# Moving a left-query pass from one kind of segment to the next in a recurrent-memory attention kernel

## The chip, the cores and the metric

The kernel runs on one core of a Trainium2 chip. The metric is the device time of one execution in microseconds; of several runs the median is given. Five engines of the core work side by side and wait for each other by semaphores: PE multiplies matrices into PSUM, ACT and DVE do elementwise work and take results out of PSUM, POOL and SP here mostly start transfers (DMA), which 16 DMA engines carry out.

## The reference, cut to what matters

The input is layer-normalised. One branch is a dense layer with GELU (1024 to 3584 and back), computed first. The other branch is attention with a recurrent memory, and takes most of the time. The 2048 rows are cut into 64 segments of 32 rows. To each segment 8 memory rows are put in front; queries, keys and values of 32 heads of 128 are made of these 40 rows; after a masked softmax and the output product, the results of the 8 memory rows are the next segment's memory:

```python
for s in range(n_seg):
    h = concatenate([mem, x[s]])           # 8 + 32 rows of 1024
    q, k, v = h @ Wq, h @ Wk, h @ Wv       # 32 heads of 128
    p = softmax(where(mask, q @ k.T * scale, -1e9))
    o = (p @ v) @ Wo
    mem, out[s] = o[:8], o[8:]
```

So segments can't run side by side: the memory that comes out of one goes into the next. The four weight matrices, 8 MB each, pass through PE once for every segment.

## The kernel before, in words

*Rows.* A matmul of 32 rows on the left uses a quarter of PE's columns, and four such matmuls run side by side. The main tile of a segment therefore has 32 rows: 24 of its own rows (NX) and the 8 memory rows. The other 8 rows of each segment, the "left" rows (NL), need no memory for their queries, keys and values. Those of four segments (GRP) make a second tile of 32 rows, `hL`, and their products are made once for a group of four segments, ahead of the group that uses them. A segment's place in its group, `i4`, is its kind, 0 to 3.

*Weights.* The weights are cut into 64 units of 128x2048 (512 KB): 8 for each of the half passes K0, Q0, K1, Q1, V0, V1, and 16 for the output pass O. 46 units stay in SBUF. 18 are streamed in every segment (the S in `PLACED`): 16 come from HBM on SP's queue, one of them in part, and two are kept in four PSUM banks and copied out by DVE (`copy_bits`). Streamed units go through 6 buffers. `unit_done` starts the next transfer into a buffer as soon as PE has used what was in it, so SP's queue goes strictly in the order in which units are used, some six units ahead.

*A segment.* `half_pass` makes one half pass: for each of 8 units, `product` issues four matmuls side by side for the main tile and, where the pass also has left rows, four more with the same unit for `hL`, into a second PSUM bank. Only three PSUM banks, `acc`, go round for all these sums. Results are taken out by ACT or DVE and turned by DVE (`turn_k`, `turn_q`, `turn_qL`). Between the products, at places given in the dictionaries `at`, the attention of the two halves is woven in: `scores`, `exps`, `sums`, `values`. Then comes the output pass, which in kind 1 has 64 rows instead of 32 (`left_o`) and takes twice as long.

*Which left passes lie in which kind.* `left_k`, `left_q`, `left_v`: K0 and V1 in kind 3, K1 and V0 in the kind 0 that follows, Q0 in kind 1, Q1 in kind 2, all for the next group.

*The boundary.* At a segment's end the memory has to go from PSUM through DVE or ACT (L1134, L1130), through PE again (`put_mem`, L293), and through a DVE cast into the main tile (L297), before the next K0 pass can begin. In that time PE makes up to six left products ahead (`LEAD`, `lead_products`), of resident units alone, for the left pass of the next segment: three before `put_mem` and three after. They keep one of the three banks until that pass is done, and the pass then makes only the two products of streamed units. Before the change each of the four kinds has such products at its end: Q0, Q1, K0, K1.

*Left queries.* `turn_qL` puts the left queries of a half, for all four segments of the next group, into `qL[u]`. This tile still holds those of the current group, so `keep_q` first copies the slots still needed into a corner of the PSUM bank `mixed` (`qS`), and `q_left` fetches a segment's 8 rows from there or from `qL[u]`. Q0's queries are overwritten in kind 1, so slots 2 and 3 are kept; Q1's in kind 2, so slot 3.

*Order.* The engines run their instructions in the order of this program; nothing is rearranged by a scheduler.

Of the kernel before, what the change touches and what calls it, by code (L numbers as in the profile page):

```python
# [11 lines left out]
U32 = mybir.dt.uint32  # L12
# [26 lines left out]
NL = SEG - NX  # L39
GRP = 4  # L40
# [49 lines left out]
def kernel(  # L90
# [63 lines left out]
    def slab(place):  # L154
        if place in low:
            return low[place]
        return slabs.tile([P, 2048], BF16, name="u", tag=place)
# [3 lines left out]
    qL = [consts.tile([P, 16, SEG], BF16, name="qL"), qL_last]  # L161
# [6 lines left out]
    for j in range(4):  # L168
        q = slice(32 * j, 32 * j + 32)
# [73 lines left out]
    def copy_bits(out, in_):  # L243

        nc.vector.tensor_single_scalar(out=out, in_=in_, scalar=0, op=ALU.bitwise_or)  # L245
# [40 lines left out]
    def put_mem(o_sb, hT, ps, nb=4):  # L286

        nc_ = KT // nb
        rows = ident_mem[:, :, :] if nb == 4 else ident_mem[:, 1::2, :]
        psM = ps[:, 0:8 * KT].rearrange("p (c j t) -> p c j t", c=nc_, j=nb)  # L290
        for c in range(nc_):
            for q in range(4):
                nc.tensor.matmul(  # L293
                    psM[32 * q:32 * q + 32, c, :, :], lhsT=o_sb[:, 4 * c + q, :], rhs=rows,
                    start=(c == 0), stop=True, skip_group_check=True, tile_position=(0, 32 * q),
                )
        nc.vector.tensor_copy(  # L297
            out=hT[:, :, NX:SEG].rearrange("p (j c) t -> p j c t", c=nc_),
            in_=psM.rearrange("p c j t -> p j c t"),
        )  # L300
# [3 lines left out]
    with tc.tile_pool(name="ma", bufs=2) as ma, tc.tile_pool(name="mps", bufs=6, space=PSUM) as mps:  # L304
# [39 lines left out]
        for i in range(14):  # L344
            t = slab(f"w2_{i}")[:, :].rearrange("p (c d) -> p c d", d=DM)
# [174 lines left out]
        for tg in range(4):  # L520
            last = tg == 3
            if last:
# [3 lines left out]
                h = 4 * IN_BANKS[1] + 2 * IN_BANKS[2]  # L526
# [12 lines left out]
            for fb in range(FC):  # L539
# [10 lines left out]
                u = ma.tile([P, 512], BF16, name="g_u")  # L550
# [99 lines left out]
    with tc.tile_pool(name="late", bufs=1) as late, \  # L650
# [10 lines left out]
        def new_acc():  # L661
            bank = free_banks.popleft()
            ps = banks.tile([P, 512], F32, name="acc", tag=bank)
            bank_of[id(ps)] = bank, ps
            return ps
# [4 lines left out]
        mixed = banks.tile([P, 512], F32, name="mixed")  # L670
# [4 lines left out]
        qS = there[:, 0:32 * NL].rearrange("p (i h t) -> p i h t", i=2, h=16)  # L675
# [12 lines left out]
        def unit_tile(unit):  # L688
            nonlocal used
            if IS_STREAMED[unit]:  # L690
                place_in_stream[unit] = used
                used += 1
                return stream_tiles.pop(used - 1)[:, :]
            return res_tiles[unit]
# [25 lines left out]
        for s in range(NSEG):  # L720
            g, i4 = divmod(s, GRP)
            first, final = s == 0, s + 1 == NSEG
# [5 lines left out]

            more = g + 1 < NGRP
            left_k = [first or (i4 == 3 and more), i4 == 0]  # L730
            left_q = [first or (i4 == 1 and more), first or (i4 == 2 and more)]
            left_v = [i4 == 0, first or (i4 == 3 and more)]
            left_o = i4 == 1 or final
            og, slot = divmod(s + 2, GRP)
# [18 lines left out]
            def lead_products(n):  # L753

                w, u, psL, ahead, order = led["next"]
                for _ in range(n):
                    if led["made"] < len(ahead):
                        i = ahead[led["made"]]
                        product(w, i, res_tiles[w, i, u], hL, psL, order)
                        led["made"] += 1  # L760
# [63 lines left out]

            def q_left(u):

                if i4 >= 2 + u and more:
                    q = qS[:, i4 - 2 - u, :, :]
                else:
                    q = qL[u][:, :, NL * i4:NL * i4 + NL]  # L830
                nc.vector.tensor_copy(out=q_home[:, :, 0:NL], in_=q)
# [4 lines left out]

            def keep_q(u):

                n = 2 - u
                copy_bits(  # L840
                    mixed[:, 340:340 + 64 * n].bitcast(U32).rearrange("p (i h t) -> p h i t", i=n, h=16),
                    qL[u].bitcast(U32)[:, :, (GRP - n) * NL // 2:].rearrange("p h (i t) -> p h i t", i=n),
                )

            def scores(u):
# [170 lines left out]
            if first:  # L1016
                keep(IN_BANKS, 1024, d_oL, 2)
                keep(IN_BANKS, 0, half_home[:, 0:DM], 3)
                h = 4 * PART[1] + 2 * PART[2]
# [7 lines left out]
            if first:  # L1027
                turn_kL(psKL, 0)
            at = {} if first else {1: [lambda: q_left(0)]}
            if left_q[0] and not first:  # L1030
                at[2] = [lambda: keep_q(0)]
            psQ, psQL = half_pass("Q", 0, left_q[0], at)
            if first:
                turn_qL(psQL, 0)
                q_left(0)
            turn_q(psQ)
            if left_q[0] and not first:
                turn_qL(psQL, 0)
            psK1, psK1L = half_pass("K", 1, left_k[1], {7: [lambda: scores(0)]})
            exps(0, None if first else lambda: q_left(1))  # L1040
            st["kT", 1] = nat_home
            rows_out(psK1, nat_home, nc.scalar.copy)
# [5 lines left out]
            if left_q[1] and not first:  # L1048
                at[0].insert(0, lambda: keep_q(1))
# [60 lines left out]
            for n, unit in enumerate(O_UNITS):  # L1110
                t = unit_tile(unit)
# [13 lines left out]
            if not final:  # L1125
                o_sb = outM
                no = 16 if left_o else 8
                o = psX[:, 0:32 * no].rearrange("p (h e) -> p h e", e=32)
                if left_o:
                    nc.scalar.copy(out=o_sb[:, 0:no, :], in_=o)  # L1130
                else:
                    o = psX[:, 0:256].rearrange("p (h e) -> p h e", e=16)
                    flat = o_sb.rearrange("p h e -> p (h e)")[:, 0:256].rearrange("p (h e) -> p h e", e=16)
                    nc.vector.tensor_tensor(out=flat, in0=o, in1=st["folded"], op=ALU.add)  # L1134
                ahead = []
                if (i4 == 3 or more) and not final:
                    hL = nxt["hL"]
                    w, u = (("Q", 0), ("Q", 1), ("K", 0), ("K", 1))[i4]
                    ahead = [i for i in range(KT) if not IS_STREAMED[w, i, u]][:LEAD]
                    order = ahead + [i for i in range(KT) if i not in ahead]  # L1140
                    led.update(next=(w, u, new_acc(), ahead, order), made=0)
                    lead_products(LEAD // 2)
                put_mem(o_sb, nxt["hT"], mixed[:, 224:288], 4 // nw)
                if led:
                    lead_products(LEAD)
# [20 lines left out]
            if final:  # L1166
                engines = [nc.sync, nc.scalar]
                n = 0
# [57 lines left out]
```

## Time and profile before

| what | value |
|---|---|
| median of 3 runs | 1837.84 us (1831.92 to 1839.93) |
| profiled execution, its own time | 1834.89 us |
| its span, first to last instruction | 1833.2 us |
| PE busy | 1720.8 us, 94% |
| PE weight loads busy | 872.6 us, 48% |
| DVE busy | 962.2 us, 52% |
| ACT busy | 665.4 us, 36% |
| DMA queue of SP (weights) | 579.67 MB, 83.6% of 16 engines' span |
| granted PE clock | 0.998 |
| recurrent part | from about 417 us to the end |

A page of the profile covers one execution. Busy time is the union of an engine's instructions; matmuls overlap, and their ends are modelled. A row of a group of instructions names the line, the engine, the operation, and the tiles as out<-in. "Idle before" is how long the engine had stood still, and the arrow names what released it. The chain of work is followed back from the last instruction, at each step to what released it; a DMA's piece in it runs from its issue to its landing. In a stretch of time, the DMA share is the time that packets took, over 16 engines' time; it can come out a little over 1.

### The profile page before, as it was taken

What the parts mean: (1) busy time and instruction counts of PE and PEld (TensorE: products, weight loads), DVE (VectorE), ACT (ScalarE), POOL (GpSimd) and SP (SyncE); (2) the same over time, 40 slices, a digit from 0 to 9 for tenths busy, and PEclk for the clock granted to TensorE, in tenths of its full rate; (3) what the DMA queues carried; (4) which work ended last, traced back from release to release, by engine and by line L of the source; (5) the groups of instructions that cost most, each with busy time, mean ns of one, the idle gap of its engine ahead of it and who ended that gap; (6) DMA issues with size and microseconds to landing.
All of it is one profiled execution on the core that took longest, in us unless ns stands there. A gap on an engine that the chain in (4) does not pass through costs nothing.

```text
span 1833.2 us, 71272 instructions
## 1 busy us (share of the span) xinstructions
PE 1720.8 (94%) x31117; PEld 872.6 (48%) x31137; DVE 962.2 (52%) x2444; ACT 665.4 (36%) x1509; POOL 276.4 (15%) x542
## 2 busy tenths in 40 slices
PE   8999999998998999999999999999999999999997
PEld 4444444444444444554445545444445444444444
DVE  7657483805554545545455555555555454545543
ACT  6334251602333333333333334333333333333333
POOL 0000001500342111112111111111111111111111
PEclk9999999999999999999999999999999999999999
DMA  9921212769999999999999999999999999999997
GB/s 291 319 85 46 55 44 57 261 209 367 400 398 365 383 389 390 380 385 380 376 382 389 393 385 386 389 387 391 374 389 383 373 393 383 381 380 390 378 386 301
DMA packets 230821, 604.65 MB, mean 330 GB/s; under 512 B 46795, under 2 KB 86267, under 8 KB 230508
## 3 DMA queue, kind: packets, MB, share of 16 engines
q1 hardware_dynamic: 207252, 579.67, 83.6%
q0 software_dynamic: 16384, 16.64, 2.9%
q8 instruction: 244, 4.00, 0.9%
q10 hardware_dynamic: 6872, 3.78, 0.7%
q14 instruction: 69, 0.57, 0.1%
HBM read 586.02 MB, written 29.10 MB: 336 GB/s over the span
## 4 chain that ended last, share of the span: by engine, by line
PE 42%; DMA 22%; issue 3%; DVE 2%; ACT 1%; DVEq 0%; ACTq 0%; SPq 0%; POOLq 0%
PE acc L744 29%; DMA u<-Wc_V 10%; PE acc L991 9%; DMA u<-Wc_O 7%; DMA u<-Wc_Q 2%; DMA u<-Wc_K 2%; PE acc L934 1%; DVE d_oL L1012 1%; DVE u L245 1%; DMA hr_home<-hr_d 1%; PE mixed L853 1%; ACT mixed L897 1%; PE mixed L293 1%; PE mixed L859 0%; ACT q_all L1130 0%
## 5 line engine op out<-in xcount | busy, mean ns | idle before, releaser
L744 PE MATMUL acc<-u,hr_home 128*32 128x512 bf16 x11520 | 790.3, 380 | 43.7 <-DMA u<-Wc_V 17.5
L744 PEld LDWEIGHTS <-hr_home 128*32 128x32 bf16 x12288 | 334.1, 96 | 352.0 <-issue 60.2
L744 PE MATMUL acc<-u,hrL 128*32 128x512 bf16 x2880 | 247.2, 379 | 2.1 <-issue 1.0
L473 PE MATMUL ps<-u 128*128 128x512 bf16 (+1 forms) x920 | 194.4, 373 | 2.0 <-ACT u L390 2.0
L245 DVE TENSOR_SCALAR u<-kept 128x512 uint32<-128x512 uint32 x254 | 163.6, 686 | 62.0 <-PE acc L991 41.6
L795 ACT CAST d_oL<-acc 128x512 bf16<-128x512 f32 x128 | 74.6, 583 | 275.0 <-PE acc L744 275.0
L991 PE MATMUL acc<-u,q_all 128*32 128x256 bf16 (+1 forms) x2207 | 133.8, 300 | 20.0 <-DMA u<-Wc_O 15.0
L594 PE MATMUL ps<-u 128*128 128x512 bf16 x657 | 146.2, 379 | 0.8
L473 PEld LDWEIGHTS <-u 128*128 128x128 bf16 x920 | 89.8, 98 | 104.9 <-issue 2.4
L1188 POOL DMA_DIRECT2D out_dram<-hr_home x188 | 96.3, 513 | 260.8 <-DVE hr_home L1154 247.0
L991 PE MATMUL acc<-u,d_oL 128*32 128x512 bf16 (+1 forms) x1536 | 131.6, 382 | 1.2 <-DMA u<-Wc_O 0.7
L907 DVE TENSOR_TENSOR pd_main<-half_home,mixed 128x320 bf16<-128x320 bf16 x128 | 62.4, 488 | 132.2 <-ACT mixed L897 132.2
L809 DVE STREAM_TRANSPOSE q_all<-q_all 128x512 bf16<-128x512 bf16 x128 | 90.6, 708 | 71.1 <-ACT q_all L795 71.0
L991 PEld LDWEIGHTS <-q_all 128*32 128x32 bf16 x3381 | 99.8, 96 | 58.9 <-issue 27.9
L799 ACT CAST q_all<-acc 128x512 bf16<-128x512 f32 x128 | 75.2, 587 | 139.1 <-PE mixed L859 138.7
L267 POOL DMA_DIRECT2D hr_home<-hr_d x58 | 32.8, 565 | 591.0 <-PE acc L744 572.6
L744 PEld LDWEIGHTS <-hrL 128*32 128x32 bf16 x3072 | 84.9, 96 | 51.3 <-issue 7.6
L795 ACT CAST q_all<-acc 128x512 bf16<-128x512 f32 x128 | 75.2, 587 | 93.5 <-PE acc L744 93.5
L594 PEld LDWEIGHTS <-u 128*128 128x128 bf16 x672 | 65.3, 98 | 77.3 <-DVE g_u L555 0.4
L897 ACT ACTIVATE mixed<-mixed,small_consts 128x160 f32<-128x160 f32 x256 | 94.3, 368 | 8.4
L547 ACT ACTIVATE g_xb<-ps,b1col 128x512 bf16<-128x512 f32 x112 | 76.8, 686 | 55.5 <-PE ps L473 54.7
L991 PEld LDWEIGHTS <-d_oL 128*32 128x32 bf16 (+1 forms) x2048 | 65.5, 99 | 59.1 <-issue 12.2
(137 smaller groups left out, 2104.6 us busy)
## 6 DMA issues: line engine op xcount, KB each, us to landing
u<-Wc_K SPq DMA_DIRECT2D x256, 512.0 KB
u<-Wc_V SPq DMA_DIRECT2D x256, 512.0 KB
u<-Wc_O SPq DMA_DIRECT2D x256, 512.0 KB
u<-Wc_Q SPq DMA_DIRECT2D x192, 512.0 KB
u<-in_B_w_dram SPq DMA_DIRECT2D x28, 512.0 KB
u<-Wc_O SPq DMA_DIRECT2D x64, 192.0 KB
hr_home<-hr_d POOLq DMA_DIRECT2D x58, 128.0 KB, 5.3
u<-in_A_Wq_dram SPq DMA_DIRECT2D x13, 512.0 KB
```

The costliest lines, as they stand in the source:

```text
L245: nc.vector.tensor_single_scalar(out=out, in_=in_, scalar=0, op=ALU.bitwise_or)
L473: nc.tensor.matmul(ps[:, SEG * s0:SEG * s1].rearrange("p (s t) -> p s t", t=SEG), lhsT=w1_sb[fb // 2][:, kt, (fb % 2) * P:(fb % 2 + 1) * P ...
L547: nc.scalar.activation(out=xb[:, :], in_=ps[:, :], func=ACT.Identity, bias=b1col[:, fb:fb + 1], scale=1.0)
L594: nc.tensor.matmul(ps[:, :], lhsT=gts[fc // 4][:, fc % 4, t * P:(t + 1) * P], rhs=w2_sb[fc // 2][:, fc % 2, cs], start=(fc == 0), stop=(fc ...
L744: nc.tensor.matmul(o, lhsT=lhs[:, i, :], rhs=m, start=(i == seq[0]), stop=(i == seq[-1]), tile_position=(0, 32 * j),)
L795: cp(out=out, in_=ps.rearrange("p (h e) -> p h e", e=32))
L799: cp(out=t[:, :], in_=ps[:, :])
L809: nc.vector.transpose(out=home, in_=home)
L897: nc.scalar.activation(out=mixed[:, 160 * b:160 * b + 160], in_=mixed[:, 0:160], func=ACT.Exp, scale=-1.0, bias=off[:, b:b + 1],)
L907: nc.vector.tensor_tensor(out=pdA.rearrange("p c b q -> p b c q"), in0=prA[:, None, :, :].to_broadcast([P, 2, 4, 40]), in1=dd, op=ALU.mult,)
L991: nc.tensor.matmul(acc[r0:r0 + rows, c:c + wide], lhsT=lhsT, skip_group_check=True, rhs=cols, start=start, stop=stop, tile_position=(0, r0),)
L1188: nc.gpsimd.dma_start(out=out_flat[rows, 256 * j:256 * j + 256], in_=res[32 * j:32 * j + NX, :])
```

## The change

Both halves' left queries are made in kind 2, none in kind 1. Kind 1 has no left half pass any more and only its longer output pass. Q0's two products of streamed units move from kind 1's Q0 pass to kind 2's. Since products ahead are made for the next segment only, and only one half pass can have them, the end of kind 0 has none now; at the end of kind 1 they are Q0's, at the ends of kinds 2 and 3 K0's and K1's as before; Q1 is made whole in its own pass. Both tiles `qL` are now overwritten in kind 2, so one slot of each half is kept in PSUM, each at its own place, and only kind 3 reads from there.

```diff
-            left_q = [first or (i4 == 1 and more), first or (i4 == 2 and more)]
+            left_q = [first or (i4 == 2 and more)] * 2
...
             def q_left(u):
 
-                if i4 >= 2 + u and more:
-                    q = qS[:, i4 - 2 - u, :, :]
+                if i4 == 3 and more:
+                    q = qS[:, u, :, :]
...
             def keep_q(u):
 
-                n = 2 - u
                 copy_bits(
-                    mixed[:, 340:340 + 64 * n].bitcast(U32).rearrange("p (i h t) -> p h i t", i=n, h=16),
-                    qL[u].bitcast(U32)[:, :, (GRP - n) * NL // 2:].rearrange("p h (i t) -> p h i t", i=n),
+                    mixed[:, 340 + 64 * u:404 + 64 * u].bitcast(U32).rearrange("p (h t) -> p h t", h=16),
+                    qL[u].bitcast(U32)[:, :, (GRP - 1) * NL // 2:],
                 )
...
-                if (i4 == 3 or more) and not final:
+                if i4 and (i4 == 3 or more):
                     hL = nxt["hL"]
-                    w, u = (("Q", 0), ("Q", 1), ("K", 0), ("K", 1))[i4]
+                    w, u = (("Q", 0), ("K", 0), ("K", 1))[i4 - 1]
```

The last condition stands inside the branch of segments that are not the final one, as before.

## The prediction

> **What bounds the kernel now.** I read the page first, then stretches of the trace cut at the end of the memory cast L297 (a segment runs from one such cast to the next), then the waits of the matmul engine, then the chain of work that ended last, and last the timeline of one boundary. Engines, and the DMA queue of the streamed weights:
>
> ```profile
> PE 1720.8 (94%) x31117; PEld 872.6 (48%) x31137; DVE 962.2 (52%) x2444; ACT 665.4 (36%) x1509; POOL 276.4 (15%) x542
> ...
> q1 hardware_dynamic: 207252, 579.67, 83.6%
> ```
>
> PE looks like the bound, but that queue alone fills 84% of a span whose first quarter hardly uses it. So both must be read by stage. One group, kinds 0, 1, 2, 3 in order (duration, then busy time and count by engine, clock, DMA share, GB/s):
>
> ```profile
> 866.50:888.61 22.11, 20.83 (x476) 10.92 (x468) 11.63 (x29) 7.99 (x20) 2.60 (x5) 1.00 1.02 392
> 888.61:912.23 23.62, 21.82 (x453) 10.70 (x450) 10.59 (x29) 7.42 (x18) 3.15 (x6) 1.00 0.99 376
> 912.23:933.14 20.91, 18.69 (x444) 9.89 (x436) 12.18 (x33) 7.57 (x19) 4.12 (x8) 1.00 1.01 383
> 933.14:955.11 21.97, 20.91 (x476) 10.86 (x468) 10.84 (x29) 8.48 (x21) 3.24 (x6) 1.00 0.97 364
> ```
>
> Over 14 groups the means are 21.81, 23.34, 20.70, 21.67 us with PE busy 20.28, 22.10, 18.61, 20.70: kind 2 has the idle PE (2.1 us), while the DMA share is about 1 in all four. What the idle PE waits for, the two largest in the whole span (total us, times, longest):
>
> ```profile
> PE acc L744 <- DMA u<-Wc_V: 17.5, 38, 1.8
> PE acc L991 <- DMA u<-Wc_O: 15.8, 33, 1.5
> ```
>
> Taken segment by segment, waits for a streamed unit cost 0.37, 0.34, 1.39 and 0.24 us in kinds 0 to 3. The chain that ended last, from kind 1 into kind 3:
>
> ```profile
> 889.61 5.31 PE acc L744 x92
> ...
> 911.93 5.44 PE acc L744 x100
> 917.39 8.07 DMA u<-Wc_V
> ...
> 927.33 7.12 DMA u<-Wc_K
> ```
>
> The chain is PE's from 889.61, through kind 1 and the K0, Q0 and most of the K1 pass of kind 2, until the slot freed at 917.39. From there it is the transfer's: issued 917.39, landed 925.46, eight microseconds of queueing behind five others. The DMA engines in kind 2, by 5 us:
>
> ```profile
> 910.00:915.00 5.00, 4.91 (x110) 2.33 (x102) 2.15 (x6) 1.17 (x2) 1.11 (x2) 1.00 0.86 303
> 915.00:920.00 5.00, 5.00 (x132) 2.80 (x128) 2.87 (x8) 1.85 (x5) 0.02 (x1) 1.00 1.02 360
> 920.00:925.00 5.00, 4.25 (x112) 2.01 (x104) 3.45 (x9) 2.37 (x6) 2.43 (x5) 1.00 1.03 413
> 925.00:930.00 5.00, 3.98 (x84) 2.03 (x84) 1.46 (x5) 2.25 (x7) 0.56 (x1) 1.00 1.03 408
> ```
>
> They idle only around the start of kind 2 (share 0.86: all six slots full after the slow output pass of kind 1), and then run at 410 GB/s while PE waits.
>
> **What the skill says.** The Trainium skill, "Perfetto Trace Analysis", section "Identifying the Most-Contended Engine", calls matmul busy time a poor measure and weight-load busy share a good one; the trace agrees: 94% against 48%. Its section "Optimization Strategy" says the most contended engine can change from regime to regime, and to interleave those; here kind 1 is PE's and late kind 2 the DMA's. "DMA: Bandwidth & Descriptors", section "Issuing engines are not separate DMA queues": SP, ACT and POOL transfers share the same 16 engines; its section "Where 436 GB/s comes from" puts the port ceiling at 435 GB/s. The 413 GB/s above, at share 1.03, is close to it. I price the streams by the trace.
>
> **The change part by part, per group (15 groups have it).** A product is four matmuls side by side: 76 matmuls took 4.27 us from 913.50, less one matmul of 0.38, so 18 steps in 3.89 us, 0.216 each. A left half is eight products, 1.73 us: six ahead at the boundary (1.30), two in the pass (0.43).
>
> *Kind 0, its end.* The six Q0 products ahead go. The boundary, PE and DVE alone:
>
> ```profile
> 975.50 0.83 PE L744 MATMUL acc<-u,hrL 128*32 128x512 bf16 x12
> 976.09 0.42 DVE L1134 TENSOR_TENSOR q_all<-acc,d_oL 128x256 bf16<-128x256 f32 x1
> 976.57 0.23 PE L293 MATMUL mixed<-ident_mem,q_all 128*32 128x32 bf16 x8 [0.23 <-DVE q_all L1134]
> 976.63 0.82 PE L744 MATMUL acc<-u,hrL 128*32 128x512 bf16 x12
> 976.85 0.23 DVE L297 CAST hr_home<-mixed 128x64 bf16<-128x64 f32 x1 [0.34 <-PE mixed L293]
> 977.28 0.39 PE L744 MATMUL acc<-u,hr_home 128*32 128x512 bf16 x4
> ```
>
> The memory chain sets it: PE waits 0.23 for DVE even with products ahead, and the next pass starts 0.20 after the cast; at 888.67, where the cast was late, it came 0.06 after. So the free filling of 1.30 is lost and the boundary shortens by only 0.14.
>
> *Kind 1.* The pass loses two streamed products, -0.43. DVE loses the bit copy (0.283), cast (0.652) and transpose (0.711) of Q0, 1.65 us; it is busy 10.42 of 23.34 here, so nothing for that. At its end six products ahead stay, of Q0 instead of Q1: 0.
>
> *Kind 2.* Before, its passes hold two products of Q1 (0.43). After, two of Q0 (0.43) and all eight of Q1, which has none ahead now (1.73): +1.73. Over the group the work is the same, -1.30 - 0.43 + 1.73 = 0; what changes is how much of it is covered. DVE gains 0.228 + 0.652 + 0.711 = 1.59 and goes from 12.19 to 13.8 of 20.7; the copies of left queries read SBUF (0.153 or 0.182) where they read PSUM (0.199). Behind the moved cast and transpose stand the masks and the K1 transpose, for which the sums in the Q1 pass wait; that pass is now twice as long, and sums come 1.07 later, so 0. Banks: Q1's left bank is the one that the Q0 cast frees. In kind 1 that cast ended at 895.19 and Q1 began at 895.45, its left product would come 0.22 later: cover 0.47, price 0 to 0.65 (one cast) if gone; I take 0.
>
> *Transfers.* Bytes and order are the same. Slots freed in Q1 come up to 1.73 later. SP has the later issues queued behind, but five units (some 6 us) stand in the DMA queue then, so the engines should not run dry; bounds 0 to +0.6, a third of the shift; I take +0.1. First use of the left rows moves a segment later; waits for their load are 0.9 us in the whole span.
>
> *Sum.* PE alone: -0.14 - 0.43 + 1.73 = +1.16. But late kind 2 waits for landings that do not move: of 1.73, 1.39 is waited there today, so PE ends kind 2 0.34 late. Kind 3's waits (0.24) take some 0.2 of it. Kind 1's saving is mostly waited away at its V units (0.34 of waits there, and landings are the DMA's); I count -0.1 of the 0.43 and 0 of the 0.14, bounds -0.57 to 0. So 0.34 - 0.2 - 0.1 + 0.1 = +0.14 a group, 15 x 0.14 = +2.1 us. The profiled execution took 1834.9 (span 1833.2), so 1837.0; on the median of the runs, 1837.84, it is **1840.0**. No change within 0.5% (9.2 us), which is about what a measurement of this kernel can tell from none.
>
> **Rivals.**
> *PE becomes the bound (slower).* Lost filling is paid in full where kind 2's waits do not go away, because the landings move with the slots or the masks, banks or issues of kind 2 keep PE from using them. Full price +1.16 x 15 = 17.4, 1855.2; it is over 0.5% once more than 0.61 of the 1.16 a group stays. For it: PE has only some 5.8 us idle a group of 87.5, and the balance loses 1.3 of free filling. Against: the 8 us of queue.
> *The lighter kind 1 counts (faster).* The chain is PE's through kind 1, so -0.43 and -0.14 there start kind 2 earlier and fill the dip of 0.86; with kind 2's addition all hidden, -0.57 x 15 = -8.6; with some 0.1 of dip regained as well, -10, 1827.8. Against: two products come back in Q0 of kind 2 before 917.39, on the same chain.
> *DVE and banks in kind 2.* Q1's left product waits for the Q0 cast: up to 0.65 x 15 = 9.8 more, if the 0.47 of cover is gone; 1849.8 at most.
> That nothing moves is ruled out by the diff; the number of left products stays 768.
>
> **Chances.** Forecast 0.60 (own range 1834 to 1846), PE-bound 0.22, kind 1 counts 0.14, DVE and banks 0.04, of which 0.03 beyond 0.5%. Faster 0.14, same 0.61, slower 0.25. For 8 in 10 the range goes to the fast rival's 1828 and most of the way to the PE bound, 1853.
>
> **What would show it.** Right: no products on the left rows at the end of kind 0, and put_mem's wait for L1134 there 0.2 to 0.9; kind 2 near 21.0 with its weight waits down from 1.39 to below 0.4; kind 1 about 23.2 with more waits for V; DMA share still 1; bit copies of left queries all 128x64. Wrong: kind 2 over 21.6 with waits still there (landings moved), DMA share under 0.97 in its V and O stages, PE gaps by qL casts at Q1, or kind 1 shorter by 0.4 and the group with it.

## The result, and the profile after

| | before | after |
|---|---|---|
| median of 6 interleaved runs each | 1838.91 us | 1847.61 us |
| ratio, 95% interval | | 1.0056 (1.0035 to 1.0078) |
| profiled execution, its span | 1834.89, 1833.2 us | 1847.1, 1845.4 us |

The kernel became slower by 10.3 us on the ratio, 0.69 us for each of the 15 groups. The changed kernel was timed once more among the experiments (label `e11_after_again`): 1.0047 (1.0028 to 1.0065), 8.6 us, 0.58 a group; one of its 22 executions, at 8454 us, is left out of this ratio. The forecast was 1840.0, the range 1828 to 1853: the time lies in the range, but four to five times as far above the kernel before as the forecast, and 1.6 us above the forecast's own range, 1834 to 1846. In the profile after, the lines behind `keep_q` are one lower (L1133 for L1134, L990 for L991).

The head of the page after, engines and the stream's queue, answers to the first lines shown of before:

```profile
PE 1720.2 (93%) x31117; PEld 876.1 (47%) x31137; DVE 960.3 (52%) x2444; ACT 666.1 (36%) x1509; POOL 276.5 (15%) x542
...
q1 hardware_dynamic: 207252, 579.67, 83.6%
```

Same instructions on PE, same bytes: the work is indeed the same, and all of the difference is time in which PE stood still. One group, kinds 0 to 3 (duration, busy time and count by engine, clock, DMA share, GB/s), cut as before at the end of L297:

```profile
873.13:895.72 22.59, 19.00 (x452) 10.21 (x444) 11.62 (x29) 8.07 (x20) 2.59 (x5) 1.00 1.01 381
895.72:918.63 22.91, 21.34 (x442) 10.81 (x442) 9.20 (x25) 7.43 (x18) 3.16 (x6) 1.00 1.01 393
918.63:939.30 20.67, 19.91 (x476) 11.01 (x468) 13.33 (x36) 7.58 (x19) 4.12 (x8) 1.00 1.00 373
939.30:961.32 22.02, 20.95 (x472) 10.80 (x468) 10.83 (x29) 8.54 (x21) 3.24 (x6) 1.00 0.99 380
```

Kind 0 has 24 matmuls fewer than the 476 before (its six products), kind 2 has 32 more than its 444, and PE's idle time there has gone from 2.2 to 0.8 us. One group proves little, so the same cuts were made for all 62 whole segments of each profile, and the waits of PE for a streamed unit added up in each (means, us; "own" is the segment without these waits; counted over the first and last groups too, the waits before come out a few hundredths off those of the prediction):

| | kind 0 | kind 1 | kind 2 | kind 3 | group | waits | own |
|---|---|---|---|---|---|---|---|
| before: segment | 21.80 | 23.22 | 20.71 | 21.65 | 87.38 | | 85.00 |
| before: waits | 0.35 | 0.33 | 1.45 | 0.25 | | 2.38 | |
| after: segment | 22.07 | 23.06 | 21.14 | 22.02 | 88.28 | | 86.06 |
| after: waits | 0.63 | 0.56 | 0.64 | 0.39 | | 2.23 | |
| after, second profile: segment | 21.95 | 22.77 | 21.44 | 21.83 | 87.98 | | 86.27 |
| after, second profile: waits | 0.38 | 0.48 | 0.45 | 0.40 | | 1.71 | |

PE's own time rose by 1.06 and 1.27 (forecast 1.16). Kind 2's waits fell by 0.81 and 1.00, which the forecast counted on. But the waits of kinds 0, 1 and 3 rose from 0.93 together to 1.58 and 1.26, where the forecast had them fall. One profile is one execution, and such sums vary: in the kernel before with six free products left out (`e2_before_without_six`, below, as fast as before), the same three kinds wait 1.19 us and the group 2.70. So 0.3 us is not beyond what a single profile can be off, and the rise stands less firmly than the times. PE's waits over the whole span (total us, times, longest), of the kernel before and of the one after:

```profile
PE acc L744 <- DMA u<-Wc_V: 17.5, 38, 1.8
PE acc L991 <- DMA u<-Wc_O: 15.8, 33, 1.5
...
PE mixed L293 <- DVE q_all L1134: 6.8, 25, 0.9
PE acc L744 <- DMA u<-Wc_Q: 6.2, 12, 1.4
...
PE acc L744 <- DVE hr_home L297: 4.2, 5, 2.9
...
PE acc L744 <- DMA u<-Wc_K: 0.8, 1, 0.8
```

```profile
PE mixed L293 <- DVE q_all L1133: 16.7, 32, 0.9
PE acc L744 <- DMA u<-Wc_V: 12.9, 32, 1.8
PE acc L990 <- DMA u<-Wc_O: 12.2, 28, 1.3
PE acc L744 <- DVE hr_home L297: 10.9, 20, 3.3
...
PE acc L744 <- DMA u<-Wc_Q: 8.3, 16, 1.7
...
PE acc L744 <- DMA u<-Wc_K: 4.6, 9, 0.9
```

Waits for V and O, where kind 2 had its waits, fell from 33.3 to 25.1 us; those for Q and K, in the first half of a segment, rose from 7.0 to 12.9. The second profile has the first (22.9), but hardly the second (7.4). And PE now waits 10 us more at the boundary of kind 0, for the DVE sum that it used to cover with left products, and 6.7 us more for the cast after it. That boundary, PE and DVE, answers to the one shown before:

```profile
982.84 0.42 DVE L1133 TENSOR_TENSOR q_all<-acc,d_oL 128x256 bf16<-128x256 f32 x1
983.31 0.12 PEld L293 LDWEIGHTS <-q_all 128*32 128x32 bf16 x8 [1.16 <-DVE q_all L1133]
983.32 0.23 PE L293 MATMUL mixed<-ident_mem,q_all 128*32 128x32 bf16 x8 [0.88 <-DVE q_all L1133]
983.60 0.23 DVE L297 CAST hr_home<-mixed 128x64 bf16<-128x64 f32 x1 [0.34 <-PE mixed L293]
...
983.88 0.40 PE L744 MATMUL acc<-u,hr_home 128*32 128x512 bf16 x4 [0.34 <-DVE hr_home L297]
```

No left product is in it; PE waits 0.88 for the sum and starts 0.05 after the cast (before: 0.20). From the last output product to the first product of the next segment it is 1.44 us in the median, before 1.59: the boundary itself is shorter by 0.15, as forecast.

The chain that ended last, from kind 2 into kind 3:

```profile
918.33 6.28 PE acc L744 x116
924.84 2.23 PE acc L744 x40
...
927.17 3.23 PE acc L744 x59
930.45 6.32 DMA u<-Wc_O
...
942.82 7.20 DMA u<-Wc_V
```

PE carries it through K0, Q0, K1, Q1 and V0, to 930.45, 11.8 us into kind 2. In the group shown of before, the transfer took over at 917.39, 5.2 us into it and ahead of Q1. There Q1's products lay beside the chain; here they lie on it, and the transfer that it goes over to is one that PE released only after them. The DMA engines over kind 2, by 5 us, cut as before:

```profile
916.40:921.40 5.00, 4.91 (x110) 2.37 (x102) 2.15 (x6) 1.17 (x2) 1.11 (x2) 1.00 0.95 319
921.40:926.40 5.00, 5.00 (x124) 2.78 (x120) 3.64 (x11) 1.42 (x3) 1.25 (x3) 1.00 1.00 362
926.40:931.40 5.00, 5.00 (x131) 2.79 (x120) 3.05 (x7) 2.21 (x6) 1.20 (x3) 1.00 1.03 411
931.40:936.40 5.00, 4.64 (x108) 2.42 (x105) 2.43 (x8) 3.02 (x10) 0.56 (x1) 1.00 1.02 369
```

The last cut has 369 GB/s where before it had 408, and its share still says 1.02. Over all groups, from 60 to 85% of kind 2's length the stream moved 406 GB/s before, at a share of 1.03, and 365 after, at 1.00 (381 at 1.01 in the second profile). The share hardly shows that a tenth of the rate is missing. The traces also tell how many transfers were on their way, from each issue to the last semaphore update of its landing. Just ahead of that stretch, from 40 to 60% of kind 2's length (the end of Q1 and V0 in the group shown), there were 5.4 before, and 4.2 and 4.3 in the two profiles after.

### The profile page after: what moved, and what is told of

Same layout as the page of the kernel before. It is cut to its first block, busy times and chain, and to the rows that moved or that the text cites. A ratio compares the mean times of both kernels' runs of the same rounds, so it can differ in the third digit from the quotient of the medians.

```text
span 1845.4 us, 71257 instructions
## 1 busy us (share of the span) xinstructions
PE 1720.2 (93%) x31117; PEld 876.1 (47%) x31137; DVE 960.3 (52%) x2444; ACT 666.1 (36%) x1509; POOL 276.5 (15%) x542
## 4 chain that ended last, share of the span: by engine, by line
PE 43%; DMA 21%; issue 3%; DVE 2%; ACT 1%; SPq 0%; DVEq 0%; ACTq 0%; POOLq 0%
PE acc L744 30%; PE acc L990 9%; DMA u<-Wc_V 9%; DMA u<-Wc_Q 4%; DMA u<-Wc_K 3%; DMA u<-Wc_O 3%; PE acc L933 2%; DMA hr_home<-hr_d 1%; DVE d_oL L1011 1%; PE mixed L852 1%; DVE u L245 1%; PE mixed L858 1%; PE acc L939 0%; ACT q_all L1129 0%; ACT mixed L896 0%
## 5 line engine op out<-in xcount | busy, mean ns | idle before, releaser
L744 PE MATMUL acc<-u,hr_home 128*32 128x512 bf16 x11520 | 806.9, 380 | 48.6 <-DMA u<-Wc_V 12.9
L744 PE MATMUL acc<-u,hrL 128*32 128x512 bf16 x2880 | 258.8, 379 | 1.9 <-issue 1.8
L990 PE MATMUL acc<-u,q_all 128*32 128x256 bf16 (+1 forms) x2207 | 132.9, 300 | 18.7 <-DMA u<-Wc_O 11.8
L990 PE MATMUL acc<-u,d_oL 128*32 128x512 bf16 (+1 forms) x1536 | 130.2, 381 | 1.3 <-issue 1.0
L990 PEld LDWEIGHTS <-q_all 128*32 128x32 bf16 x3381 | 99.5, 96 | 58.5 <-ACT q_all L955 26.2
L990 PEld LDWEIGHTS <-d_oL 128*32 128x32 bf16 (+1 forms) x2048 | 65.1, 99 | 58.3 <-issue 10.1
```

Source lines behind the costliest of these rows:

```text
L744: nc.tensor.matmul(o, lhsT=lhs[:, i, :], rhs=m, start=(i == seq[0]), stop=(i == seq[-1]), tile_position=(0, 32 * j),)
L990: nc.tensor.matmul(acc[r0:r0 + rows, c:c + wide], lhsT=lhsT, skip_group_check=True, rhs=cols, start=start, stop=stop, tile_position=(0, r0),)
```

## The experiments

Two theories were set against each other. *Depth*: slots that Q1 frees late leave fewer transfers in flight, the stream then moves less although its share stays at 1, and the later segments wait for it. *Fixed landings*: what the forecast said, that landings do not move. Beside these stood *DVE and banks*: Q1's left product held up by the moved casts. All ratios below are to the kernel before, run on the same chip beside each experiment; 0.001 is 0.12 us a group.

**The six products alone.** In the changed kernel, the six left products of resident units are left out of the Q1 pass of kind 2, so the left queries of Q1 come from two units only; all else stays.

```diff
                     psL = new_acc()
+                    if (w, u) == ("Q", 1) and not first:
+                        order = [i for i in order if IS_STREAMED[w, i, u]]
...
-                    if left and i not in ahead:
+                    if left and i in order and i not in ahead:
```

> The changed kernel, with the six left products of resident units left out of the Q1 pass of kind 2 (they aren't made anywhere, so 1.30 us of PE work a group is missing; the two of streamed units stay). Depth theory (the rate of the weight stream falls with the number of transfers in flight, and products in Q1 that hold PE up keep landed units in their slots): back to the kernel before or a little under it, ratio 0.997 to 1.001. Theory of fixed landings (the stream runs at one rate as long as its queue isn't empty, so the 1.30 us were hidden behind weight waits and the loss comes from elsewhere): hardly a change against the changed kernel, 1.004 to 1.006. Theory of DVE and banks in kind 2 (the second cast and transpose are what costs): stays at 1.004 to 1.006 too, since both stay.

In the kernel before, the six products ahead at the end of kind 0 (Q0's) are left out instead.

```diff
                     order = ahead + [i for i in range(KT) if i not in ahead]
+                    if i4 == 0:
+                        order = [i for i in order if i not in ahead]
+                        ahead = []
```

> The kernel before, with the six Q0 products ahead left out at the end of kind 0 (they aren't made anywhere; the two of streamed units in kind 1 stay). All theories: these products were free, the boundary shortens by the 0.14 us that the first pass waited for PE, 2 us in all, ratio 0.998 to 1.000. If it falls under 0.996, they were not free.

| | ratio | 95% interval |
|---|---|---|
| after, without Q1's six in the pass | 0.9989 | 0.9967 to 1.0011 |
| before, without Q0's six at the boundary | 1.0003 | 0.9984 to 1.0021 |

The changed kernel without these six is no slower than the kernel before; they are 1.0056 - 0.9989 = 0.0067, 12.3 us or 0.82 a group of the 1.30 that they take on PE (0.71 by the second measurement, 1.0047). Its moved casts, copies and transposes, its banks and kind 1's lighter pass are all still there, so *DVE and banks* has nothing left to explain; nor does any wait of PE in the two profiles after name a cast of left queries. Fixed landings, under which the six would have been mostly waited away, falls. In this run's trace kind 2 has 5.2 transfers on their way from 40 to 60% of its length and 406 GB/s from 60 to 85%, nearly as before: what is missing from the stream after goes with the six products. At the boundary six such products were worth nothing measurable: the filling there was free, as the forecast had it.

**The same step in two places.** In the kernel before, with all its work, six products ahead are moved into the pass that follows: once Q0's, from the end of kind 0 into kind 1, once Q1's, from the end of kind 1 into kind 2.

```diff
+                    if i4 == 0:
+                        ahead, order = [], list(range(KT))
```

> The kernel before, with the six Q0 products made in the Q0 pass of kind 1 and not ahead at the end of kind 0 (all work is done). Theory of fixed landings: 0.34 us of weight waits follow in kind 1, the rest of 1.16 us is paid, 0.8 a group, 12 us, ratio 1.006 to 1.008. Depth theory: much the same or a little more, since PE is behind the landings from there to the middle of kind 2, 1.006 to 1.010. It tells what lost filling costs where PE is the bound.

```diff
-                if (i4 == 3 or more) and not final:
+                if i4 != 1 and (i4 == 3 or more) and not final:
```

> The kernel before, with the six Q1 products made in the Q1 pass of kind 2 and not ahead at the end of kind 1; Q0 stays in kind 1 with its products ahead (all work is done). So kind 2's Q1 pass is that of the changed kernel, but with one cast and transpose of left queries in kind 2. Depth theory: as the changed kernel, 1.004 to 1.008. Theory of fixed landings: 1.30 - 0.14 of work against 1.39 of waits, 1.000 to 1.001. Theory of DVE and banks: 1.000 to 1.001, since kind 2 has no second cast.

| | ratio | 95% interval | a group | own | waits |
|---|---|---|---|---|---|
| before | 1 | | | 85.00 | 2.38 |
| Q0's six into kind 1 | 1.0039 | 1.0022 to 1.0057 | 0.48 us | 85.62 | 2.08 |
| Q1's six into kind 2 | 1.0036 | 1.0021 to 1.0051 | 0.44 us | 86.12 | 1.69 |

The second is most of what the change does to kind 2, with nothing moved out of kind 1. Its profile has kind 2's waits at 0.61, as after, with 4.8 transfers on their way and then 391 GB/s in the same two stretches. The loss rejects fixed landings (1.000 to 1.001), but is a little under what depth asked for (1.004 to 1.008). The first is the bigger miss: kind 1, which had seemed to be PE's alone, with 0.33 of waits, should have passed on nearly all of the six products; 0.48 of 1.16 (1.30 less the 0.14 of the boundary) came through, and both theories had asked for more (1.006 to 1.008, 1.006 to 1.010). In its profile even PE's own time rose by 0.62 only, which is not explained. Neither place hides the step, neither charges it in full. Whether the change costs more than the step of Q1 alone (1.0047 and 1.0056 against 1.0036) is not settled: the intervals overlap.

**Fewer buffers.** One of the six stream buffers of the kernel before is not used.

```diff
                 start_stream("xn2")
-                start_stream("xn3")
```

> The kernel before with five stream buffers instead of six (all work is done). Depth theory: some 3.8 instead of 4.8 transfers in flight, so by the trace of before about 365 instead of 388 GB/s, 6% longer in the recurrent part: ratio 1.03 to 1.06. Theory of fixed landings: the queue still never runs empty (four in flight), so hardly longer, 1.000 to 1.010.

It measured 1.0543 (1.0505 to 1.0581), 6.6 us a group. Waits of PE in its profile, and one of its kind 2 segments:

```profile
PE acc L990 <- DMA u<-Wc_O: 49.7, 88, 1.9
PE acc L990 <- DVE u L245: 47.1, 44, 1.7
PE acc L743 <- DMA u<-Wc_V: 43.4, 94, 1.8
```

```profile
1137.88:1160.95 23.07, 19.35 (x444) 9.76 (x436) 12.29 (x32) 7.57 (x19) 4.14 (x8) 1.00 0.99 359
```

In this segment the DMA share is 0.99 at 359 GB/s. In the profile the group is 6.8 us longer. Waits for streamed units rose by 4.6 of it, from 2.38 to 6.94. Not all the rest is the stream: 47 us, 3.1 a group, are waits for DVE's copies of kept units into the buffers, which come late as well, and smaller idle times went. So depth works downward: the time lies where depth expected it, though the waits for the stream are only two thirds of it.

**The stream by itself.** A kernel with nothing but 64 transfers of 512 KB through 1, then 2, up to 6 buffers; each is used up by one tiny DVE copy, and nothing of the reference is computed.

```diff
+    for depth in range(1, 7):
...
+        for m in range(TURNS):
+            t = tiles.pop(m)
+            nc.vector.tensor_copy(out=acc[:, 0:16], in_=t[:, 0:16])
+            if m + depth < TURNS:
+                issue(m + depth)
```

> The weight stream alone: 64 transfers of 512 KB through 1, then 2, 3, 4, 5 and 6 buffers, each buffer freed by a small DVE copy as soon as its transfer has landed; nothing of the computation is made, and the output is not the reference's. Depth theory: the rate still rises from 4 to 6 in flight, by over 3%. Theory of fixed landings: the rate is flat within 1% from 3 on.

Stretches of its trace, 48 transfers each, for 1 to 6 buffers in order (duration, DVE and POOL busy, clock, DMA share, GB/s):

```profile
62.47:230.77 168.30, 8.23 (x49) 0.00 (x0) 1.00 0.43 150
275.76:381.46 105.70, 8.24 (x49) 0.00 (x0) 1.00 0.74 238
414.25:495.72 81.47, 8.25 (x48) 0.00 (x0) 1.00 0.88 307
522.74:588.06 65.32, 8.24 (x48) 0.00 (x0) 1.00 1.00 382
608.53:670.36 61.83, 8.25 (x48) 0.00 (x0) 1.00 1.03 410
690.83:753.10 62.27, 8.23 (x48) 0.00 (x0) 1.00 1.03 409
```

With four in flight the share is already 1.00, but the rate is 7% below that with five. Five and six are equal. So the rate is not flat from three on, as fixed landings needed. The trace of the kernel before shows the same in itself: cut into stretches of 1 us, with 3, 4, 5 and 6 transfers on their way, it moved 318, 371, 394 and 408 GB/s at shares of 0.90, 0.99, 1.02 and 1.03, and 4.8 were on their way in the mean, six in a fifth of the time only. So this stream is most of the time on the slope, not at the ceiling.

**A seventh buffer.** There is no room for one; it was got by giving the resident unit at the place `w2_13` the tile of the one at `w2_12`, so in these kernels the weights of the one stand in for those of the other; the multiplications are as many as before. Before and after, first with nothing else changed, then with `LATER`, the number of places by which the copies of kept units start late, raised from 3 to 4:

```diff
-LATER = 3
+LATER = 4
...
+            if place == "w2_13":
+                res_tiles[unit] = res_tiles[UNIT_AT["w2_12"]]
+                start_stream(place)
+                continue
```

> The kernel before with a seventh stream buffer. Its room comes from one resident output unit, for which another unit's weights are used, so its share of the result is wrong, while every matmul is still made. Depth theory: over five in flight, rate above 400 GB/s, most of the 2.3 us of weight waits a group go: ratio 0.975 to 0.990. Theory of fixed landings: the rate is the same, 0.997 to 1.000.

> The changed kernel with a seventh stream buffer, made in the same way. Depth theory: now PE is the bound, and the lost filling is paid nearly in full, 0.8 to 1.2 us a group over the seven-buffer kernel before, 12 to 18 us, ratio to that kernel 1.007 to 1.010; to the kernel before 0.983 to 0.999. Theory of fixed landings: the six-buffer difference stays, 1.004 to 1.006 over the seven-buffer kernel before.

> The kernel before with seven stream buffers as in the run before (one output unit's weights stand in for another's, so a share of the result is wrong; every matmul is made), and with the two units kept in PSUM started four places late instead of three, so that DVE copies them out where it did with six buffers, and not ahead of the memory chain. Depth theory: the weight waits go and nothing takes their place; PE's own time of some 85.0 us a group is left of 87.4, 36 us less, ratio 0.978 to 0.988. Theory that the stream has one rate whatever is in flight: 0.997 to 1.002.

> The changed kernel, in the same way. Depth theory: PE is the bound nearly everywhere, and of the lost filling of 1.16 us a group more is paid than with six buffers: 0.9 to 1.2, 14 to 18 us over the seven-buffer kernel, ratio to that one 1.008 to 1.010. If kind 2's buffers had been the reason for the loss, and a seventh buffer removes it: 1.000 to 1.003.

| | ratio | 95% interval |
|---|---|---|
| before, seven buffers, LATER 3 | 1.0029 | 1.0015 to 1.0043 |
| after, seven buffers, LATER 3 | 1.0087 | 1.0057 to 1.0117 |
| before, seven buffers, LATER 4 | 0.9894 | 0.9854 to 0.9934 |
| after, seven buffers, LATER 4 | 0.9944 | 0.9925 to 0.9963 |

The first pair misses what depth expected of it (0.975 to 0.990 for the kernel before, 0.983 to 0.999 for the one after), and is no test of it. Weight waits were nearly gone in the kernel before (0.94 a group), and in their place stood this wait, 6.8 us in the whole span with six buffers:

```profile
PE mixed L297 <- DVE q_all L1138: 60.6, 47, 2.0
```

With one buffer more, everything starts one place earlier, and DVE's copy of a kept unit (1.29 us) came to lie ahead of the memory sum at the end of the segments. The second kernel of this pair, moreover, had a mean granted clock of 0.987 against 0.995. The second pair puts the copies back where they were. The later start itself was not run with six buffers for both kept units. Now the seventh buffer gains 1.1%, a little less than expected, and the weight waits are at 0.43 a group; in the profiled execution, at 1828.87 us the slowest of its six, much of the idle time is put down to PE's own issue instead (24.3 us in all at the products, with six buffers 10.5). Between its two kernels lies 0.9944 / 0.9894 = 1.0050, with an interval of about 1.0006 to 1.0095 from the two above. That holds both a loss as with six buffers and next to none, and its middle lies between the two expectations (1.008 to 1.010, 1.000 to 1.003), so whether a deeper queue hides the change's cost stays open.

**Kept copies later.** Of the two kept units, only that of the Q0 pass is started one place later in the kernel before, to see whether the shift of copies alone has any worth.

```diff
-        LATER if unit == IN_BANKS or (unit == IN_PSUM and n >= STREAMED) else 0 for n, unit in enumerate(streams)
+        LATER if unit == IN_BANKS else LATER + 1 if unit == IN_PSUM and n >= STREAMED else 0
+        for n, unit in enumerate(streams)
```

> The kernel before, with the unit of the Q0 pass that is kept in PSUM started four places late instead of three (all work is done), so that a buffer holds it some 0.6 us less in each segment and a transfer has its place. Depth theory: 2.5 us of buffer time a group, at 6.8 us for the 87 us of a whole buffer (five against six) 0.2 us a group, 3 us, ratio 0.997 to 0.999, unless PE then waits for the copy, which is ready some 0.2 us before its use: 1.000 to 1.004.

0.9991 (0.9971 to 1.0012): nothing that can be measured. The changed kernel was also run again, unedited:

> The changed kernel once more, for a narrower interval beside the kernel before, and to set it against the one that has only Q1 in its pass (1.0036): all of the loss is lost filling: 1.003 to 1.005; a part is due to Q0's move into kind 2: 1.005 to 1.008.

1.0047 (1.0028 to 1.0065), as told above. No kernel here that computes the whole reference is faster than the kernel before.

## Why the prediction was right and wrong

The wide range holds the time because it had been stretched over the rivals; the sum behind the forecast did not lead there. Point by point, by its own steps:

- *Sum of PE's own time, +1.16*: right, as far as two profiles can tell. Measured +1.06 and +1.27.
- *Kind 0, boundary shorter by 0.14, the free filling of 1.30 lost*: right. It is 0.15 shorter, its wait for L1133 is 0.79 us in the mean (forecast 0.2 to 0.9), and leaving the six out there was worth nothing (1.0003).
- *Kind 1, -0.43, mostly waited away*: right in kind. The segment is 0.16 and 0.45 shorter, its waits 0.23 and 0.15 longer. Only in the second profile does it reach the 0.4 that the forecast named as a sign against it, and the group is longer all the same.
- *DVE and banks in kind 2, 0*: right; the kernel without the six, with these all in place, is at 0.9989, and no wait for such a cast shows after.
- *Late kind 2 waits for landings that do not move; of 1.73, 1.39 is waited there today*: this is the step that failed. Kind 2's waits did fall, by 0.8 to 1.0 of the 1.39, to 0.64 and 0.45 (forecast below 0.4). Kind 2 is 21.14 and 21.44 long, under the 21.6 that was to show the PE-bound rival. But the landings moved. Slots freed late in Q1 start their transfers late, with 4.2 and 4.3 on their way instead of 5.4; the stream moves 6 to 10% less late in kind 2, and in part for what kind 2 no longer waits, the other kinds wait more, 0.65 and 0.33 us a group, where the forecast subtracted 0.2 in kind 3.
- *Transfers, +0.1 with bounds 0 to +0.6, because the engines should not run dry*: the term of the sum that was mis-sized. Against the forecast's +0.14 a group, the runs paid 0.58 and 0.69, so this term, with kind 3's waits, is about +0.45 to +0.55 more: close to its upper bound. The reason given was a share of 1 with five units queued. The engines did not run dry, and yet they moved less. The Trainium skill, "Perfetto Trace Analysis", section "Identifying the Most-Contended Engine", says to judge the DMA by the HBM's utilization and not by occupancy, which 16 engines make misleading. The forecast cited that section for PE, and passed over this sentence; the runs agree with it (share 1.00 at 382 GB/s, 1.03 at 410).
- *Signs to look for*: "DMA share still 1" came true and meant nothing; GB/s in kind 2's V and O stages was the sign, and it fell.
- *Rivals*: of the 1.16 a group, 0.58 to 0.69 stays, half of the full price of the PE-bound rival, and just at the 0.61 from which it was to count as slower by over 0.5%. Its reason, "the landings move with the slots", is what was found; its "in full" is not.

That the six products in Q1 cost time is shown, by leaving them out; that fewer buffers and fewer transfers on their way cost time, by the five buffers and the stream alone. That the six make the stream move less late in kind 2 is read from the traces with and without them. That this is what makes kinds 0, 1 and 3 wait is argued, from the rates and waits in the profiles. Not explained is why about half is paid, neither all nor nothing, and why kind 1 paid no more than kind 2. An estimate from the rates of 60 to 85% of kind 2: what the stream moved less there than before (365, 381 and 391 for 406 GB/s, over some 5.3 us) takes it about 0.55, 0.35 and 0.2 us at a mean of some 390 GB/s, for 0.69, 0.58 and 0.44 that were paid in the changed kernel, its second measurement and the one with Q1's six alone. So the order fits and the amount falls short. Over the whole group the transfers on their way (4.8 before, 4.7 and 4.75 after) hardly differ.

## What to carry to other kernels

A wait for a transfer is slack only as far as the transfer was started by something that you don't delay: where a buffer's release starts the next load, work added ahead of the release can cost time even before a wait that seemed long enough to hide it, here about half of its own. Judge a stream by its GB/s in the stage and by how many transfers are on their way, against a run of the stream alone, rather than by the busy share of the DMA engines. And products that fill a wait on a serial chain cost nothing measurable there, while the same products inside a pass did cost here, in whichever of two passes they were put.

## What the hardware showed that was not expected

- One core's stream of 512 KB transfers from SP's queue needs five on their way for its full 410 GB/s, though one at a time they follow each other every 3.5 us (168.30 / 48, the small copy between them included), and with four the share is already 1.00.
- In this kernel buffers are also held while they are used, so that the sixth, which is worth nothing to the stream alone, is worth 5.4%, and a seventh, with the kept copies started one place later, another 1.1%.
- That seventh is lost again (1.0029) when 1.29 us of DVE work comes to lie ahead of the memory sum, at three of the four boundaries of a group.
